# A new order of work per engine, pair sums on VectorE and a bf16 softmax in a two-branch token-mixing kernel

## The chip, the cores and the metric

One Trainium2 chip, one core. The metric is the device time of one execution in microseconds (us). Before the change it was 210.38 us (median of 3 runs, 210.28 to 210.64). The executions of before agree within about 0.3%. A run that is more than 1.5% above the fastest run of the same kernel is called slow and kept out of the comparisons.

Engine names: PE is TensorE (matmuls), PEld its weight loads, DVE VectorE, ACT ScalarE, POOL GpSimd, SP SyncE, which here only issues transfers.

## The reference, cut to what matters

```python
# x (1, 2048, 512) bf16; 32 heads of 16; window of 8 keys, dilation 2; Fh = 688
xn = layernorm(x)
# A: local attention
q, k, v = split(xn @ wqkv)                       # per head
logits[s, w] = q[s] . k[s - 2*w] / 4,  w = 0..7  # masked where s - 2*w < 0
o = softmax(logits) applied to v[s - 2*w];  A = o @ wo
# B: gated mixing over the tokens
z = gelu(xn @ w_in);  z1 = z[:, :688];  z2 = layernorm(z[:, 688:])
g = w_sp @ z2 + b_sp                             # w_sp is 2048 x 2048: the largest product
B = (z1 * g) @ w_out
out = x + A + B
```

The kernel works on 16 tiles of 128 tokens. "Tile n" below is the n-th in the kernel's own order.

## The kernel before: the parts that matter

The logits are made by DVE, which multiplies q by shifted k over all 512 channels, and by PE, which adds up each head's 16 channels with a 0/1 matrix. The channels lie in four chunks of 128, so each group of logits takes four passes of PE.

```python
NWSP = 6                                   # homes for transposed tiles of w_sp
NZ1 = 8                                    # slots for z1 and u = z1 * g
...
def logits(g):
    pl = ps_aux.tile([P, 4, P], F32, name="pl", tag="aux")
    for c in range(C):                     # C = 4 chunks
        for tb in range(TB):
            PE.matmul(pl[32 * tb:32 * tb + 32, :, :], rsel[:, c, :], pr[g % 2][:, c, :, tb, :],
                      start=(c == 0), stop=(c == C - 1), tile_position=(0, 32 * tb))
    A.activation(lg[:, 4 * h:4 * h + 4, o, :], pl[:], ACT.Copy, scale=float(DH) ** -0.5)
```

The gelu of z1 tile n writes slot n % 8. `u_mul` multiplies g into the same slot. A DMA transpose on SP's queue then reads that slot into `uT`, from where PE uses it as weights:

```python
def z1_mm(n):
    pz = zmm(i, w_z1)                                      # PE, into a PSUM buffer (3 of them)
    A.activation(z1u[:, n % NZ1, z:z + FH]..., pz[:, :, 0:FHALF], ACT.Gelu_apprx_tanh)

def u_mul(n, gs):
    s = n % NZ1
    V.tensor_tensor(z1u[:, s, 0:FULL], g[:, 0:FULL], z1u[:, s, z:z + FULL], ALU.mult)
    ...
    SP.dma_start_transpose(uT[:, (n // 4) % 2, :, ...], z1u[:, s, :])   # directly behind the multiply
```

The order is a plain program. The weights `wo` (2 MB in all, because four copies go to four partition groups) are issued ahead of the loop:

```python
for tb in range(TB):
    SP.dma_start(wo_r[32 * tb:32 * tb + 32, :, :], A_wo.rearrange("(h d) n -> h d n", d=DH))
load_xr(0)
...
for n in range(NT):
    if n >= 4:
        z1_mm(n)
    gs = g_mm(n)
    if n in OUT_AFTER: outs(n)             # an output block of 4 tiles, then its next residual loads
    for _ in range(APPLY_PER_G[n]):
        ap.pop(0)()                        # attention applies on DVE
    u_mul(n, gs)
    ...
    if n + NWSP < NT:
        load_wsp(n + NWSP)                 # DMA transpose of one tile of w_sp
out_mm(3, last=True)
```

## Time and profile before

| | value | where |
|---|---|---|
| time | 210.38 us, span of the profiled run 209.3 us | runs, page |
| PE busy | 202.7 us, 97% | page, part 1 |
| first q/k matmul | 8.46 us | timeline |
| last matmul ends | 206.0 us, 3.3 us before the end | stretches |
| DVE, ACT busy | 176.9, 92.9 us | page, part 1 |

Three lines of the page before: busy time of each engine with its share of the span and number of instructions; then the span in 40 slices, a digit for the busy tenths of PE and of the clock that the throttle granted it.

```profile
PE 202.7 (97%) x1727; PEld 121.3 (58%) x1731; DVE 176.9 (85%) x267; ACT 92.9 (44%) x148; POOL 5.7 (3%) x21
...
PE   7799999999999999999999999999999999999993
...
PEclk9999999999999999999999999999999999999999
```

Busy time in three stretches of before, cut at the first q/k matmul and at the last matmul. Columns: stretch and its length, busy us of PE, PEld, DVE, ACT, POOL (instructions), mean granted clock, DMA share, GB/s.

```profile
0.00:8.46 8.46, 5.87 (x19) 2.17 (x20) 4.56 (x15) 3.09 (x6) 4.41 (x19) 1.00 0.67 203
8.46:206.00 197.54, 196.79 (x1708) 119.12 (x1711) 171.60 (x250) 89.81 (x143) 1.29 (x2) 1.00 0.57 120
206.00:209.30 3.30, 0.00 (x0) 0.00 (x0) 0.76 (x2) 0.00 (x0) 0.00 (x0) 0.90 0.37 119
```

Read the middle line first: of 197.54 us PE is busy 196.79, at full clock. PE is the limit from end to end, so only two things can shorten this kernel: less work on PE, or shorter ends. Everything else has slack, and slack can only be lost.

The group of the logits matmuls before (engine, operation, tiles, shapes, count, busy us, mean ns, idle before):

```profile
L304 PE MATMUL pl<-r_pr,rsel 128*32 128x512 bf16 x128 | 8.2, 381 | 0.0
```

The queue of SP before, around the issue of `wo`. Columns: start, duration of the issue, queue, line, operation, transfer, count.

```profile
89.63 2.92 SPq L609 DMA_DIRECT2D r_lg<-in_A_wo_dram  x4
92.60 1.91 SPq L397 DMA_DIRECT2D r_qk<-in_A_x_dram  x4
102.63 1.28 SPq L392 DMA_TRANSPOSE uT<-z1u  x1
104.02 1.96 SPq L369 DMA_TRANSPOSE r_qk<-in_B_w_sp_dram  x1
```

`wo` goes out at 89.6 us, 42 us before the output heads use it (131.39 us). The two durations of a transpose: 1.28 us for a tile of u, 1.96 us for a tile of w_sp.

### The profile page before, as it was taken

What the parts mean: (1) busy time and instruction counts of PE and PEld (TensorE: products, weight loads), DVE (VectorE), ACT (ScalarE), POOL (GpSimd) and SP (SyncE); (2) the same over time, 40 slices, a digit from 0 to 9 for tenths busy, and PEclk for the clock granted to TensorE, in tenths of its full rate; (3) what the DMA queues carried; (4) which work ended last, traced back from release to release, by engine and by line L of the source; (5) the groups of instructions that cost most, each with busy time, mean ns of one, the idle gap of its engine ahead of it and who ended that gap; (6) DMA issues with size and microseconds to landing.
All of it is one profiled execution on the core that took longest, in us unless ns stands there. A gap on an engine that the chain in (4) does not pass through costs nothing.

```text
span 209.3 us, 4186 instructions
## 1 busy us (share of the span) xinstructions
PE 202.7 (97%) x1727; PEld 121.3 (58%) x1731; DVE 176.9 (85%) x267; ACT 92.9 (44%) x148; POOL 5.7 (3%) x21
## 2 busy tenths in 40 slices
PE   7799999999999999999999999999999999999993
PEld 2578644545566566666666666456666446664441
DVE  3888997969999987999999999859999979991404
ACT  3475797788997897941431223102123102231000
POOL 7000001100000000000000000000000000000000
PEclk9999999999999999999999999999999999999999
DMA  4984556000000499799999776994833234424153
GB/s 132 326 281 66 101 94 232 0 0 3 0 3 0 103 179 210 146 280 216 177 191 218 129 161 145 147 194 150 126 76 89 47 94 150 47 45 89 51 152 100
DMA packets 66914, 25.91 MB, mean 124 GB/s; under 512 B 56080, under 2 KB 66768, under 8 KB 66768
## 3 DMA queue, kind: packets, MB, share of 16 engines
q1 hardware_dynamic: 66304, 25.20, 56.1%
q10 hardware_dynamic: 592, 0.46, 0.7%
q8 instruction: 13, 0.21, 0.4%
q14 instruction: 5, 0.04, 0.1%
HBM read 10.13 MB, written 2.10 MB: 58 GB/s over the span
## 4 chain that ended last, share of the span: by engine, by line
PE 93%; DMA 3%; SPq 2%; issue 1%; DVE 0%; DVEq 0%
PE pg L377 36%; PE pz L207 18%; PE pq L264 12%; PE po L430 7%; PE po L411 7%; PE pv L342 7%; PE pl L304 4%; DMA r_w<-in_A_wqkv_dram 3%; PE pa L430 1%; PE po L417 1%; SPq L138 1%; SPq L131 1%; SPq L147 0%; PE pt L193 0%; DVE r_qk L422 0%
## 5 line engine op out<-in xcount | busy, mean ns | idle before, releaser
L377 PE MATMUL pg<-z,r_qk 128*128 128x344 bf16 x512 | 76.8, 309 | 0.0
L377 PEld LDWEIGHTS <-r_qk 128*128 128x128 bf16 x512 | 50.0, 98 | 24.9 <-issue 0.4
L207 PE MATMUL pz<-w_z,xnT 128*128 128x344 bf16 x256 | 40.9, 309 | 0.0
L380 ACT ACTIVATE gs<-pg,b_col 128x688 bf16<-128x688 f32 x16 | 13.3, 832 | 57.0 <-PE pg L377 50.1
L353 DVE TENSOR_TENSOR r_pr<-r_x,r_w 128x2048 bf16<-128x2048 bf16 x32 | 38.1, 1221 | 0.3
L357 DVE TENSOR_TENSOR r_pr<-r_pr 128x2048 bf16<-128x2048 bf16 x28 | 33.8, 1219 | 0.1
L207 PEld LDWEIGHTS <-xnT 128*128 128x128 bf16 x256 | 24.6, 98 | 14.7 <-issue 2.0
L264 PE MATMUL pq<-xnT,r_w 128*128 128x256 bf16 (+1 forms) x176 | 29.4, 321 | 0.8 <-ACT xnT L197 0.7
L297 DVE TENSOR_TENSOR r_pr<-r_qk 128x2048 bf16<-128x2048 bf16 x24 | 27.5, 1218 | 2.8 <-ACT r_qk L269 2.8
L264 PEld LDWEIGHTS <-r_w 128*128 128x128 bf16 x176 | 16.8, 98 | 11.5 <-issue 1.8
L422 DVE TENSOR_TENSOR r_qk<-po,r_qk 128x512 bf16<-128x512 f32 x14 | 9.0, 686 | 15.6 <-PE po L430 15.6
L256 ACT ACTIVATE z1u<-pz 128x688 bf16<-128x688 f32 x16 | 11.9, 742 | 20.8 <-PE pz L207 20.7
L269 ACT CAST r_qk<-pq 128x1024 bf16<-128x1024 f32 x16 | 15.8, 1012 | 5.8 <-PE pq L264 4.3
L430 PE MATMUL po<-r_w,uT 128*128 128x512 bf16 x66 | 14.9, 379 | 0.6 <-issue 0.6
L342 PE MATMUL pv<-xnT,r_w 128*32 128x512 bf16 x256 | 14.7, 380 | 0.0
L411 PE MATMUL po<-r_lg,r_pr 32*128 32x512 bf16 x224 | 14.5, 375 | 0.0
L430 PEld LDWEIGHTS <-uT 128*128 128x128 bf16 x80 | 7.5, 98 | 10.2 <-issue 1.7
L175 DVE BATCH_NORM_STATS2 stats<-r_x 128x6 f32<-128x512 bf16 x16 | 10.8, 672 | 2.3 <-DMA r_x<-in_A_x_dram 2.1
L219 ACT ACTIVATE junk<-z 128x688 bf16<-128x688 bf16 x16 | 12.4, 778 | 0.5
L213 ACT ACTIVATE z<-pz 128x688 bf16<-128x688 f32 x16 | 11.8, 736 | 1.9 <-PE pz L207 1.9
L342 PEld LDWEIGHTS <-r_w 128*32 128x32 bf16 x256 | 9.5, 139 | 4.5 <-issue 0.3
L411 PEld LDWEIGHTS <-r_pr 32*128 32x128 bf16 x256 | 6.2, 93 | 7.7 <-issue 1.3
(67 smaller groups left out, 136.3 us busy)
## 6 DMA issues: line engine op xcount, KB each, us to landing
r_lg<-in_A_wo_dram SPq DMA_DIRECT2D x4, 512.0 KB, 9.0
r_qk<-in_A_x_dram SPq DMA_DIRECT2D x16, 128.0 KB, 2.2
out_dram<-r_qk SPq DMA_DIRECT2D x15, 128.0 KB, 1.7
r_x<-in_A_x_dram SPq DMA_DIRECT2D x3, 512.0 KB, 6.0
w_z<-in_B_w_in_dram SPq DMA_DIRECT2D x2, 688.0 KB, 5.3
r_w<-in_A_wqkv_dram SPq DMA_DIRECT2D x4, 256.0 KB, 6.4
r_w<-in_B_w_out_dram SPq DMA_DIRECT2D x1, 640.0 KB, 5.6
r_w<-in_A_wqkv_dram SPq DMA_DIRECT2D x1, 512.0 KB, 4.0
```

Source lines behind the costliest of these rows:

```text
L207: PE.matmul(pz[:, hh, 0:FHALF], xnT[:, kc, i * P:(i + 1) * P], wz[:, kc, hh * FHALF:(hh + 1) * FHALF], start=(kc == 0), stop=(kc == C - 1))
L219: A.activation(junk[:], z2[:, i, :], ACT.Square, accum_out=zsq[:, q:q + 1])
L264: PE.matmul(pq[:, s, b0 * P:b1 * P], wqk[:, kc, s * D + c * P:s * D + (c + 1) * P], xv[:, kc, b0:b1, j, :], start=(kc == 0), stop=(kc == C ...
L269: A.copy(dst[:, :, :, j, :], pq[:].rearrange("p s (b t) -> p s b t", b=TB))
L297: V.tensor_tensor(pr[g % 2][:, :, ww], q4, k4, ALU.mult)
L342: PE.matmul(pv[32 * tb:32 * tb + 32, dd, :], wv[:, kc, 2 * d2 + dd, :], xnT[:, kc, tb * TBS:(tb + 1) * TBS], start=(kc == 0), stop=(kc == ...
L353: V.tensor_tensor(pw_t[n], vp[:, :, off:off + P], a_sb[:, slot_w(w), ts].unsqueeze(1).broadcast_to([P, DH, P]), ALU.mult)
L357: V.tensor_tensor(pw_t[n] if dst is None else dst, pw_t[n], pw_t[m], ALU.add)
L377: PE.matmul(pg[:, hh, 0:FHALF], wsp[n % NWSP][:, k, :], z2[:, k, hh * FHALF:(hh + 1) * FHALF], start=(q == 0), stop=(q == NT - 1))
L380: A.activation(gs[:], pg[:, :, 0:FHALF], ACT.Identity, bias=b_col[:, i:i + 1])
L411: PE.matmul(pos[tb], op[32 * tb:32 * tb + 32, d, o * P:(o + 1) * P], wo_r[32 * tb:32 * tb + 32, d, :], start=(d == 0), stop=False, tile_po ...
L430: PE.matmul(pos[tb], uT[:, o % 2, m, tb * P:(tb + 1) * P], wout[:, m, :], start=False, stop=(m == MCH - 3))
```

## The change

The intent: halve PE's work for the logits, which is PE time, by letting DVE first add the four chunks in pairs; make room on DVE with a bf16 softmax and with a reciprocal taken on ACT as exp(-ln); and place every single step of z2, q/k, softmax, v, g, applies and outputs by a list, so that PE always finds its inputs. The w_sp tiles get separate homes. As before, `wo` can be issued only after the second softmax exponential, because its home is the logits' buffer; that exponential now ends at about 119 us. The bf16 logits fill only the lower half of the buffer, and two w_sp tiles use the upper half for a time.

```diff
-NWSP = 6
-APPLY_PER_G = [1, 2, 3, 4, 4, 4, 4, 4, 4, 6, 6, 6, 4, 4, 3, 1]
-OUT_AFTER = [8, 12, 15.5]
+PAIRED = (0, 1, 2, 3, 4, 5, 6, 7)
+ORDER = """
+z0.2 z0.3 z2.2 zg0.2 p1.3 ...
+... A9 M1.1 U1 M1.2 Gi3 A10 G5 Gi9 M1.3 U3 E1 A11 T3 A12 wo X8 Gi5 S1.0 X11 A13 w11 G8 A14 Xg8 Xg11 A15 xr0 A16 U6
+T2 A17 X9 Gi8 T1 U5 S1.1 G7 A18 A19 Xg9 S1.2 A20 A21 O0 Gi7 A22 ... A24 Or0 Oh0.0 A25 U8 Oh0.1 F0.0
+A26 s0.0 w10 U7 G11 ... A31 G12 A32 xr1
+Gi10 A33 A34 T7 A35 T5 A36 X15 Gi12 s0.3 T9 A37 X12 A38 X14 Xg15 A39 Xg12 G15 ...
+... xr3 Or3 Oh3.0 Oh3.1 F3.0 F3.1 s3.1 s3.0
+"""
 NZ1 = 8
...
+    def pair_add(g):
+        V.tensor_tensor(pr[g % 3][:, 0:2], pr[g % 3][:, 0:2], pr[g % 3][:, 2:4], ALU.add)
...
-        for c in range(C):
+        n_c = 2 if g in PAIRED else C
+        for c in range(n_c):
             for tb in range(TB):
-                PE.matmul(pl[...], rsel[:, c, :], pr[g % 2][:, c, :, tb, :],
+                PE.matmul(pl[...], rsel[:], pr[g % 3][:, c, :, tb, :],
...
-        V.reciprocal(s4[:, 0, :], s4[:, 0, :])
+            A.activation(smt[:, 1, :], smt[:, 0, :], ACT.Ln)
+            A.activation(srec[:], smt[:, 1, :], ACT.Exp, scale=-1.0)
...
-    for c in range(C):
-        prod_c(0, c)
...
+    for tok in ORDER.split():
+        name = tok.rstrip("0123456789.")
+        steps[name](*[int(a) for a in tok[len(name):].split(".") if a])
```

Words of the list: `Xn` z1 matmuls of tile n, `Xgn` their gelu, `Gn` g matmuls, `Un` multiply, `Tn` DMA transpose of tile n of u, `wn` DMA transpose of tile n of w_sp, `wo` the four loads of wo, `xro` the residual loads of output block o, `Oo`, `Oro`, `Oho.h` the matmuls of output block o, `Fo.t` and `so.t` its adds and stores. Each engine takes its own steps in the order of the list; dependences between engines are added automatically. `T1`, `wo`, `w11`, `xr0` and `T2` all go through SP.

## The prediction

> **What bounds the kernel now.** TensorE. The page has PE busy 202.7 of 209.3 us, and by its waits PE never idles more than 0.2 us at a time after its first q/k matmul at 8.46 us. The stretches view: 59.97 of 59.98 us busy from 23.5 (first z2 tile) to 83.5 (first g tile), 121.8 of 122.5 from there to 206.0. Behind the last matmul is a tail of 3.3 us (add, store). Clock 1.0 throughout. DVE is busy 176.9 us, ACT 92.9 us. So only PE work removed, or the two ends, can give time; moves on other engines can only cost.
>
> **Removed from PE.** The logits reduction: 128 matmuls, 8.2 us (0.98 per group of 16). Pair sums halve them: -4.1 us. Nothing else on PE shrinks; 256-column halves and the cut last block add about 0.3 us.
>
> **Start.** The second transpose no longer stands behind two warm-up matmuls (they end at 7.35; its input was ready at 6.35), and the q weights come as one transfer issued about 0.9 us earlier. First q/k matmul perhaps 0.4 us earlier (0 to 0.7).
>
> **DVE.** Eight adds of 4096 elements: a 2048-element bf16 operation has a pitch of 1.14 us, so 2.2 each, +17.7. bf16 max, subtract and normalise at half the fp32 cost (1.22 against 2.29 us for 2048; the Trainium skill, "VectorE: DVE Perf Modes", has 2-byte tensor_tensor at two elements a cycle; the trace agrees): -6.9; reciprocal moved to ACT -3.5; one Newton chain less -2.5. DVE grows by about 5 us to 181 while the span shrinks: nearly critical.
>
> **ACT.** 10 table loads for 4. The skill ("ScalarE: Activation LUTs", What ACT_TABLE_LOAD costs) says 2.66 us with the drain; this trace shows 1.28 us and the next instruction directly after. +7.7 us, plus small Ln/Exp; ACT has room, but loads delay PSUM evacuations.
>
> **New waits.** Adding up the new order per engine with these durations, DVE first waits for q/k casts (blocks 2, 0, 3) and falls some 7 us further behind. Then: a few tenths at L5 and G0 (pair sum, z2 norms), about 1 us at L6/L7 (pair sum 7), about 0.8 at the second-last output block (uT transpose queued on SP behind the one for tile 13), little or nothing at the last head projection, which the final apply add reaches barely in time, and perhaps at O0 (2 MB of wo issued only near 99+ us). Together 2 us (1 to 5).
>
> **Tail.** On DVE the adds of the first two tiles of the last block now stand *behind* the three adds of the last two, and their two 128 KB stores leave last on SP. After the last matmul come one 224-column add, two 0.66 us adds, two issues of 0.65 us, a transfer: about 5.3 us instead of 3.3, +2 us.
>
> **Sum.** 210.4 - 4.1 - 0.4 + 0.3 + 2.0 + 2 = 210.2; I may overestimate waits, for such an order is presumably searched for: 209.2 us, 8 in 10 from 206.3 to 212.3. Faster by 2%: 0.12; within: 0.80; slower: 0.08.
>
> **What would show it.** PE busy near 199; logits group near 4.1 us; PE idle of 1 to 5 us released by DVE pair adds, z2 norms or DMA; DVE busy near 181; 10 table loads; last matmul to end about 5.3 us with two DVE adds in it.
>
> **What would make it wrong.** DVE lag larger than added up (mask, strided product slower than 1.22 us, apply adds): then all outputs slip, slower. Later x arrival through the GpSimd queue. Or no waits and an earlier start: 207.

## The result, and the profile after

The change made the kernel slower: 218.95 us (218.81, 216.94, 219.21, 219.10) against 210.51 us for before in the same rounds, a ratio of 1.0367, 95% interval 1.0318 to 1.0415. A ratio here and below is the mean time of one kernel's fast runs over that of the other's in the same rounds, so it is not quite the ratio of the medians quoted. All outputs were correct.

The same three lines of the page after:

```profile
PE 201.7 (93%) x1695; PEld 126.7 (58%) x1699; DVE 181.1 (83%) x259; ACT 100.0 (46%) x161; POOL 3.4 (2%) x15
...
PE   8899999999999999999999995499996999999990
...
PEclk9999999999999999999999999599999699999999
```

PE has two dents, at about 60% and 80% of the span, and the granted clock has one at or just behind each. Outside them PE is as full as before. What PE waited for after (engine, line, releaser: us in total, times, longest):

```profile
PE po L495 <- ACT r_uz L296: 5.4, 1, 5.4
PE pg L447 <- ACT r_uz L296: 2.4, 1, 2.4
```

Two waits, 7.8 us, both for an instruction of line 296, the gelu of z1. What that gelu waited for:

```profile
ACT r_uz L296 <- DMA r_uz<-r_uz: 9.9, 1, 9.9
```

`r_uz<-r_uz` is a DMA transpose of u: it reads a slot of u in `r_uz` and writes `uT`, in the same tensor. The queue of SP after shows why it was late; these are the lines that answer to the four of before:

```profile
117.76 1.22 SPq L467 DMA_TRANSPOSE r_uz<-r_uz  x1
119.20 1.79 SPq L642 DMA_DIRECT2D r_lg<-in_A_wo_dram  x4
121.09 10.45 SPq L438 DMA_TRANSPOSE r_qk<-in_B_w_sp_dram  x1
131.58 2.00 SPq L472 DMA_DIRECT2D r_qk<-in_A_x_dram  x4
133.63 2.56 SPq L467 DMA_TRANSPOSE r_uz<-r_uz  x2
```

The third line is the event. The issue of one w_sp transpose, 1.96 us before, held SP's queue for 10.45 us. (A wait for a semaphore lies ahead of an issue's start and is not part of this time: in e2 below an issue of 0.32 us follows a wait of 20 us.) The four `wo` transfers, issued just ahead, landed at 125.24, 127.59, 130.18 and 131.84 us; the issue ended at 131.54. The two transposes in the last line are `T2` and `T1`; `T1` landed at 137.66. Then, in time order on the other engines (start, duration, engine, line, operation; the bracket is the idle time before and what ended it):

```profile
127.95 4.83 PE L447 MATMUL pg<-z,r_qk 128*128 128x344 bf16 x32
132.71 0.39 PE L495 MATMUL po<-r_lg,r_pr 32*128 32x512 bf16 x2
137.74 0.74 ACT L296 ACTIVATE r_uz<-pz 128x688 bf16<-128x688 f32 x1 [9.87 <-DMA r_uz<-r_uz]
138.53 5.29 PE L495 MATMUL po<-r_lg,r_pr 32*128 32x512 bf16 x62 [5.44 <-ACT r_uz L296]
146.56 0.69 DVE L509 TENSOR_TENSOR r_qk<-po,r_qk 128x512 bf16<-128x512 f32 x1 [7.68 <-PE po L519]
```

Gelu 9 writes slot 9 % 8 = 1, so it must wait until `T1` has read that slot. Until gelu 9 has read its PSUM buffer, the buffer is not free. There are three of them: z1 tile 9, g tile 7, and the first of two for the output heads. After two head matmuls PE stands, until gelu 9 is done. DVE later waits 7.68 us for the first output sums.

The second dent is the same dependence with n = 15 and slot 7. `T7` was issued from 162.92 us in a pair, behind the residual loads `xr1`, landed at 166.4, and ACT then still had a table to load (1.28 us) before the gelus. PE stood 2.41 us, until 168.60:

```profile
162.92 2.59 SPq L467 DMA_TRANSPOSE r_uz<-r_uz  x2
168.60 6.50 PE L447 MATMUL pg<-z,r_qk 128*128 128x344 bf16 x32 [2.41 <-ACT r_uz L296]
```

The stretches after, cut at the first q/k matmul, around the first dent, and at the last matmul:

```profile
7.37:132.80 125.43, 125.30 (x1058) 84.15 (x1058) 115.69 (x171) 83.62 (x139) 0.81 (x2) 1.00 0.55 119
132.80:138.50 5.70, 0.30 (x2) 0.00 (x1) 5.63 (x6) 0.76 (x2) 0.00 (x0) 0.70 0.74 183
138.50:212.10 73.60, 70.50 (x617) 40.58 (x620) 53.68 (x67) 12.61 (x16) 0.00 (x0) 0.95 0.50 107
212.10:217.10 5.00, 0.00 (x0) 0.00 (x0) 1.59 (x4) 0.00 (x0) 0.00 (x0) 0.99 0.33 105
```

Up to 132.8 us nothing was lost at all: PE is busy 125.30 of 125.43 us. The first g tile starts at 81.36 us, against 83.45 before, although 4.6 us more of z matmuls lie ahead of it (192 against 160) and only 16 of the 64 logits matmuls (1.0 us) are left for later. By this estimate the change was more than 5 us ahead at that point. In the clock's own records half rate was granted from 135.12 to 141.94 and from 169.25 to 172.66 us. In both stretches about 3.41 us of it lay under matmuls, which loses half of that: an estimate of 1.7 us each. The matmul times agree: the 62 head matmuls behind the first dent took 5.29 us, all 64 of them before 3.63.

The logits after, in two tiles because a third buffer was added:

```profile
L358 PE MATMUL pl<-r_pr,rsel 128*32 128x512 bf16 x48 | 3.3, 381 | 0.0
L358 PE MATMUL pl<-r_uz,rsel 128*32 128x512 bf16 x16 | 1.2, 382 | 0.0
```

3.3 + 1.2 = 4.5 us instead of 8.2: 3.7 us less. With the spans of the two profiled runs (209.3 and 217.1) the account is as follows. PE's work is what the other terms leave; PE's busy time in the same stretch, less the half clock, gives the same (196.10 - 3.4 - 196.79 = -4.1).

| term | us | from |
|---|---|---|
| first q/k matmul earlier | -1.1 | 7.37 - 8.46 |
| PE work between first q/k and last matmul | -4.1 | (212.09 - 7.37 - 7.85 - 3.4) - 197.54; 3.7 of it logits |
| PE idle | +7.85 | 5.44 + 2.41 |
| half clock under matmuls | +3.4 | estimate from the clock records, as above |
| last matmul to the end | +1.7 | 5.0 - 3.3 |
| sum | +7.8 | 217.1 - 209.3 = 7.8 |

The start. Before, then after: the second group of transposes stood behind two warm-up matmuls; after, all eight run together.

```profile
6.29 1.06 PE L469 MATMUL pwm<-warm 128*128 128x512 bf16 x2
7.41 0.38 PE L193 MATMUL pt<-ident,r_x 128*128 128x128 bf16 x4
8.46 1.03 PE L264 MATMUL pq<-xnT,r_w 128*128 128x256 bf16 x8 [0.67 <-ACT xnT L197]
```

```profile
5.78 0.92 PE L220 MATMUL pt<-ident,r_x 128*128 128x128 bf16 x8 [0.27 <-DVE r_x L213]
6.53 0.49 PE L546 MATMUL pwm<-warm 128*128 128x512 bf16 x2
7.37 1.03 PE L305 MATMUL pq<-xnT,r_w 128*128 128x256 bf16 x8 [0.35 <-ACT xnT L224]
```

The end. Before, two additions of 256 columns are left after the last matmul, which ends at 205.97 us. After, the last matmul ends at 212.09 us; one addition of 224 columns follows, then two of 512 columns, and their stores behind them:

```profile
206.01 0.76 DVE L422 TENSOR_TENSOR r_qk<-pa,r_qk 128x256 bf16<-128x256 f32 x2 [0.27 <-PE pa L430]
```

```profile
212.12 0.39 DVE L509 TENSOR_TENSOR r_qk<-pb,r_qk 128x224 bf16<-128x224 f32 x1
212.43 1.28 DVE L509 TENSOR_TENSOR r_qk<-po,r_qk 128x512 bf16<-128x512 f32 x2
```

### The profile page after: what moved, and what is told of

Same layout as the page of the kernel before. It is cut to its first block, busy times and chain, and to the rows that moved or that the text cites. A ratio compares the mean times of both kernels' runs of the same rounds, so it can differ in the third digit from the quotient of the medians.

```text
span 217.1 us, 4082 instructions
## 1 busy us (share of the span) xinstructions
PE 201.7 (93%) x1695; PEld 126.7 (58%) x1699; DVE 181.1 (83%) x259; ACT 100.0 (46%) x161; POOL 3.4 (2%) x15
## 3 DMA queue, kind: packets, MB, share of 16 engines
HBM read 10.13 MB, written 2.10 MB: 56 GB/s over the span
## 4 chain that ended last, share of the span: by engine, by line
PE 78%; DVE 8%; DMA 6%; SPq 4%; issue 1%; ACT 1%; DVEq 0%; ACTq 0%
PE pg L447 27%; PE pz L234 16%; PE pq L305 12%; PE po L495 7%; PE pv L408 6%; PE po L519 6%; DMA r_w<-in_A_wqkv_dram 3%; DVE r_pr L422 3%; DMA r_uz<-r_uz 3%; DVE r_pr L426 2%; PE pl L358 2%; DVE r_qk L509 2%; SPq L438 2%; SPq L472 1%; PE pa L519 1%
## 5 line engine op out<-in xcount | busy, mean ns | idle before, releaser
L447 PE MATMUL pg<-z,r_qk 128*128 128x344 bf16 x448 | 68.1, 314 | 2.4 <-ACT r_uz L296 2.4
L447 PEld LDWEIGHTS <-r_qk 128*128 128x128 bf16 x448 | 44.4, 99 | 25.4 <-issue 2.6
L305 PEld LDWEIGHTS <-r_w 128*128 128x128 bf16 x184 | 20.1, 114 | 7.6 <-DMA r_w<-in_A_wqkv_dram 0.8
L315 ACT CAST r_qk<-pq 128x1024 bf16<-128x1024 f32 (+1 forms) x16 | 15.3, 991 | 4.9 <-PE pq L305 4.9
L296 ACT ACTIVATE r_uz<-pz 128x688 bf16<-128x688 f32 x16 | 11.5, 744 | 12.1 <-DMA r_uz<-r_uz 9.9
L495 PEld LDWEIGHTS <-r_pr 32*128 32x128 bf16 x272 | 8.4, 99 | 13.2 <-issue 8.7
L519 PE MATMUL po<-r_w,r_uz 128*128 128x512 bf16 x66 | 14.9, 379 | 0.6 <-issue 0.6
L350 DVE TENSOR_TENSOR r_pr<-r_pr 128x4096 bf16<-128x4096 bf16 x6 | 13.7, 2284 | 0.1
L519 PEld LDWEIGHTS <-r_uz 128*128 128x128 bf16 x85 | 8.0, 98 | 9.8 <-issue 1.5
L339 DVE TENSOR_TENSOR r_uz<-r_qk 128x2048 bf16<-128x2048 bf16 x8 | 9.7, 1220 | 3.3 <-ACT r_qk L315 3.3
```

What stands on the lines that cost most here:

```text
L305: PE.matmul(pq[:, cc, p0 * P:(p0 + b1 - b0) * P], wqk[:, sd, kc, c0 + cc:D:C], xv[:, kc, b0:b1, j, :], start=(kc == 0), stop=(kc == C - 1))
L315: cast = A.copy(dst, pq[:, :, p0 * P:(p0 + b1 - b0) * P].rearrange("p c (b t) -> p c b t", b=b1 - b0))
L339: prod = V.tensor_tensor(pr[g % 3][:, c].rearrange("p w b t -> p b w t"), q3.unsqueeze(2).broadcast_to([P, TB, 4, P]), k4, ALU.mult)
L350: V.tensor_tensor(pr[g % 3][:, 0:2], pr[g % 3][:, 0:2], pr[g % 3][:, 2:4], ALU.add)
L447: PE.matmul(pg[:, hh, 0:FHALF], wsp[n][:, k, :], z2[:, k, hh * FHALF:(hh + 1) * FHALF], start=(k == 0), stop=(k == NT - 1))
L495: PE.matmul(pc, op[32 * tb:32 * tb + 32, d, o * P:(o + 1) * P], wo_r[32 * tb:32 * tb + 32, d, cs], start=(d == 0), stop=False, tile_positi ...
```

## The experiments

Theory A: the slowdown comes from u transposes that stand too late in SP's queue, the first of them behind a w_sp transpose that the 2 MB of `wo` holds up; gelu, PSUM buffer and PE follow. Rival B: DVE is overloaded by the pair sums (181 us busy) and everything slips behind it. Rival C: the long w_sp transpose waited for PE, as the profile infers (it names z1 matmuls of line 234 as its releaser, 7.1 us; the z1 tile that ends in that time is the one that runs from 126.78 us), and `wo` has nothing to do with it. A further question is how much the order of the end costs. Ten kernels ran, all correct. The first four share one chip and its runs of before, so do e5 to e8, and so do e9 and e10. Times in the table are medians of the fast runs; one run of e1, two of e2 and one of e10 count as slow.

| run | edit, against the kernel after unless said | time us | ratio to before, 95% |
|---|---|---|---|
| after | | 218.95 | 1.0367 (1.0318 to 1.0415) |
| e1 | T2, T1 ahead of wo | 211.28 | 1.0057 (0.9996 to 1.0118) |
| e2 | wo issued by ACT | 231.02 | 1.0975 (1.0926 to 1.1024) |
| e3 | adds of the end reordered | 215.82 | 1.0281 (1.0226 to 1.0335) |
| e4 | e1 and e3 | 209.17 | 0.9939 (0.9924 to 0.9954) |
| e5 | e4, T7 and T5 early | 207.30 | 0.9839 (0.9819 to 0.9859) |
| e6 | e5 without pair sums | 210.89 | 1.0004 (0.9983 to 1.0026) |
| e7 | e5, wo in two halves | 205.55 | 0.9757 (0.9741 to 0.9774) |
| e8 | no pair sums, order as given | 220.75 | 1.0477 (1.0441 to 1.0513) |
| e9 | w11 behind T1 | 215.71 | 1.0220 (1.0156 to 1.0284) |
| e10 | wo in two halves, order as given | 212.59 | 1.0155 (1.0089 to 1.0221) |

### e1: two transposes ahead of wo

```diff
-... E1 A11 T3 A12 wo X8 ... A16 U6
-T2 A17 X9 Gi8 T1 U5 S1.1 G7 ...
+... E1 A11 T3 T2 T1 A12 wo X8 ... A16 U6
+A17 X9 Gi8 U5 S1.1 G7 ...
```

> The change as given, but the transposes of u tiles 2 and 1 stand on the SyncE queue ahead of the wo loads and of the w_sp load for tile 11; nothing else moves. Theory A (queue order: gelu 9 must wait until the transpose of u tile 1 has read its buffer, and that transpose stood behind a w_sp load whose issue took 10.45 us while 2 MB of wo were in flight): the 9.9 us wait of ScalarE for that transpose, the 5.4 us idle of TensorE before the first head projection and the 7.7 us wait of VectorE for the first output add go; the clock stays at 1.0 there; 208 to 213 us against 219. The second stall (2.4 us before g tile 15, behind the residual loads of block 1) may stay or shrink. Theory B (VectorE is overloaded by the pair adds and everything runs late): at most 1 us better, 217.5 or more.

211.28 us (211.28, 213.26, 210.58; a fourth, 215.25, counts as slow), against 218.95. The wait of the output heads for a gelu is gone. One wait of 1.5 us for `wo` itself and the wait at tile 15 (3.2 us) are left. The profiled run of this kernel is the slow one: it holds two stretches of half clock, and I read only the kinds of waits from it. The held w_sp transpose was still there, 10.58 us long (10.13 in e4 below). So the hold alone made PE wait for no gelu; what stood behind it did. This supports A and speaks against B, since DVE's work is the same.

### e2: wo through the other issuing engine

```diff
-            SP.dma_start(wo_r[32 * tb:32 * tb + 32, :, :], A_wo...)
+            A.dma_start(wo_r[32 * tb:32 * tb + 32, :, :], A_wo...)
```

> The change as given, but the four wo loads go out from ScalarE's queue; the order on SyncE's queue is unchanged. Theory A (the w_sp load for tile 11 is held at issue by the wo bytes in the same queue): its issue takes 2 to 4 us instead of 10.45, the transpose of u tile 1 is issued before 128 us of the span, the stall before the first head projection shrinks to under 1 us, 208 to 214 us. Rival C (that w_sp load waits for TensorE, as the profile's inference says: g tile 5 or the z1 tile that ends at 128.1): the load still ends near 131.5 us and the time stays within 1 us of 219.

231.02 us (230.21 and 231.83; the other two, 233.68 and 234.51, count as slow): the time missed both expectations by far, and `T1` went out at 137.5 us instead of before 128. The transpose itself answered the question. The queue of SP in e2:

```profile
119.67 3.51 SPq L438 DMA_TRANSPOSE r_qk<-in_B_w_sp_dram  x1
123.23 12.02 SPq L472 DMA_DIRECT2D r_qk<-in_A_x_dram  x4
```

It was issued by 123.18 us, in 3.51 us, although the z1 tile that C lets it wait for did not run before 142 us in this kernel (PE had stopped at 122.0). C falls, and an inferred releaser is only an inference: the hold has to do with `wo`. (The home of this w_sp tile is that of tile 5, and g tile 5, its last reader, was through at 119.9 us in the kernel after.) That `wo` must stand in the same queue is not shown, because ACT had sent off only two of the four transfers, half of the bytes, by the time the transpose was through.

The loss came from elsewhere. ACT did no work for 22.83 us, and PE idled 20.6 us at one place. The four issues themselves took only 0.32 to 0.43 us each. In the trace the third and the fourth wait for a semaphore, the counter that a transfer raises when it lands, which had last been given to a transfer of SP's queue: the third went out at 140.87 us, when the w_sp transpose had landed at 140.84, the fourth at 141.22, when the first residual load had landed at 141.18. The Trainium skill, "DMA: Bandwidth & Descriptors", section "Issuing engines are not separate DMA queues", says that transfers of all issuers interleave on the same 16 DMA engines and that using several issuers saves only sequencer time, "which is usually small". The second half agrees with these short issues, of transfers that took 5.4 to 20.5 us to land. The first half is not tested here: the residual loads beside `wo` took 12.02 us to issue, against 2.00, but they stood behind the w_sp transpose in their own queue.

### e3: the end

```diff
-... xr3 Or3 Oh3.0 Oh3.1 F3.0 F3.1 s3.1 s3.0
+... xr3 Or3 Oh3.0 F3.0 F3.1 s3.1 s3.0 Oh3.1
```

> The change as given, but the adds and stores of the first two tiles of the last output block stand before the matmuls and adds of the last two. All theories: from the last matmul to the end 3.3 to 3.6 us instead of 5.5, so 2.0 us faster (216.5 to 217.2); the stalls in the middle stay.

215.82 us (215.84, 215.80, 215.77, 218.24). The last matmul to the end is 3.4 us (210.7 to 214.1) instead of 5.0. (The 5.5 in the expectation came from a cut at 211.6 us, ahead of the last matmul.) The ratio fell by 1.0367 - 1.0281 = 0.0086, about 1.8 us. The medians differ by more, 3.1 us: in three of the four runs the mean granted clock was 0.984, against 0.975 to 0.978 in the kernel after, and the profiled one has no half clock behind its second dent. Both dents stay (5.6 and 1.3 us). So the end was a separate loss, of 1.6 us by the trace.

### e4: both repairs

> Both edits of order (u transposes 2 and 1 early; tail adds early). Theory A: the sum of the two gains, 206 to 211 us, at or under the kernel before (210.4). Theory B: 215 or more.

209.17 us (209.00 to 209.49), ratio 0.9939: both repairs add up, and the granted clock is 1.00 throughout. The queue of SP in e4, where `T2` and `T1` are already gone before `wo`:

```profile
117.41 3.91 SPq L467 DMA_TRANSPOSE r_uz<-r_uz  x3
121.43 1.91 SPq L642 DMA_DIRECT2D r_lg<-in_A_wo_dram  x4
123.44 10.13 SPq L438 DMA_TRANSPOSE r_qk<-in_B_w_sp_dram  x1
```

A wait at tile 15 is left, now 2.3 us, and 1.0 us for `wo`.

### e5: the second late transpose

```diff
 # on top of e4
-A26 s0.0 w10 U7 G11 ...  /  Gi10 A33 A34 T7 A35 T5 A36 X15 ...
+A26 s0.0 w10 U7 T7 T5 G11 ...  /  Gi10 A33 A34 A35 A36 X15 ...
```

> The two edits of order of the run before it (u transposes 2 and 1 early, tail adds early), and the transposes of u tiles 7 and 5 directly after the products of tile 7, ahead of the stores and residual loads of block 0 to 1. Theory A: the last wait of TensorE on a u transpose (2.3 us before g tile 15) goes, the 1.0 us wait for wo stays: 206.4 to 207.4 us against 209.17 without it. Theory B (VectorE late): no change, 209.

207.30 us (206.91 to 207.67), ratio 0.9839. The wait at tile 15 is gone; 1.2 us of waiting for `wo` is the only new wait left. So the second dent, too, was a u transpose issued late, and three moves of steps on SP and DVE have taken the kernel from 3.7% slower to 1.6% faster.

### e6: what the pair sums are worth

```diff
 # on top of e5
-PAIRED = (0, 1, 2, 3, 4, 5, 6, 7)
+PAIRED = ()
```

> The run before it with no pair sums: four chunks go into each logits matmul group again. If the pair sums are worth their TensorE time once nothing stalls: 4.1 us slower than e5 (210 to 211.5), minus up to 1 us if VectorE's 18 us less brings wo earlier. If VectorE were what bounds (theory B): the same as e5 or faster.

210.89 us, ratio 1.0004. Against e5 of the same rounds: (1.0004 - 0.9839) x 210.7 = 3.5 us. PE busy rises from 197.5 to 201.1 us, DVE falls from 180.9 to 163.6. PE's saving arrives in the total nearly whole, once nothing else stands in the way; DVE's 17.3 us cost nothing. The expectation that `wo` would come earlier with less work on DVE missed: it went out at 124.22 us, 121.63 in e5, and PE's wait for it grew from 1.2 to 1.8 us, so up to 0.6 of the 3.5 us may be this wait.

### e8: no pair sums in the given order

Edit: `PAIRED = ()` in the kernel after, nothing else.

> The change exactly as given, but no pair sums. Theory A: the queue order is unchanged, so gelu 9 still waits for the transpose behind the w_sp load behind wo; VectorE reaches the softmax of the second half earlier, so wo goes out up to 8 us earlier and the stall shrinks by what wo gains, while TensorE has 4.1 us more: 212 to 220 us. Theory B: VectorE's lag was the cause, so the stall is gone and the time is 209 to 212 us, TensorE never idle over 1 us.

220.75 us (2 runs), just above the 212 to 220 of theory A; ratio 1.0477. What PE waited for in e8:

```profile
PE po L495 <- ACT r_uz L296: 5.8, 1, 5.8
```

DVE was relieved of 17.4 us (163.7 busy), and the stall of 5.4 us became 5.8. B falls. One part of my own expectation missed: with DVE freed I thought `wo` would go out earlier; it went out at 121.98 us, later than with the pair sums (119.20), probably because PE then has 4 us more logits work ahead of it.

### e9: the w_sp transpose moved behind the u transposes

```diff
-... wo X8 Gi5 S1.0 X11 A13 w11 G8 ... xr0 A16 U6 T2 A17 X9 Gi8 T1 U5 ...
+... wo X8 Gi5 S1.0 X11 A13 G8 ... xr0 A16 U6 T2 A17 X9 Gi8 T1 w11 U5 ...
```

> The change as given, but the w_sp load for tile 11 stands behind the transpose of u tile 1 on SyncE's queue; wo and the four residual loads still stand ahead of it. If only the many small descriptors of a transposing load are held behind the 2 MB of wo: the residual loads and the transpose go out without delay, its landing is before 129 us, the stall before the first head projection is gone, 208 to 213 us. If whatever is issued next behind wo is held until wo has mostly moved: the residual loads or the u transposes take the 8 to 10 us instead, the stall stays over 3 us, 216 to 219 us.

215.71 us (215.38, 216.04, 213.07, 216.18), ratio 1.0220. This asks whether the w_sp transpose is special, or whether any DMA transpose directly behind `wo` is held. The queue of SP in e9:

```profile
118.85 1.79 SPq L642 DMA_DIRECT2D r_lg<-in_A_wo_dram  x4
120.68 2.37 SPq L472 DMA_DIRECT2D r_qk<-in_A_x_dram  x4
123.98 8.00 SPq L467 DMA_TRANSPOSE r_uz<-r_uz  x2
```

The plain residual loads behind `wo` went out in 2.37 us. The u transposes behind them were held, 8.00 us for two instead of 2.56, until 131.98 us; the last `wo` transfer landed at 131.41. So a transpose of u is held as well, not only one of w_sp, and plain loads in this place are not. (In e2 plain loads were slow too, behind a w_sp transpose.) Neither branch of the expectation came true as written: the residual loads went out freely, the u transposes did not, and with a stall of 2.7 us the time lay just under the second branch.

### e10: wo in two halves, in the given order

```diff
-... M1.0 w7 U2 ...  A11 T3 A12 wo X8 ...
+... M1.0 w7 wo.1 U2 ...  A11 T3 A12 wo.0 X8 ...
-    def load_wo():
+    def load_wo(h):
         for tb in range(TB):
-            SP.dma_start(wo_r[32 * tb:32 * tb + 32, :, :], A_wo.rearrange("(h d) n -> h d n", d=DH))
+            SP.dma_start(wo_r[32 * tb:32 * tb + 32, 8 * h:8 * h + 8, :],
+                         A_wo.rearrange("(h d) n -> h d n", d=DH)[:, 8 * h:8 * h + 8, :])
```

The upper half of wo's home becomes free before the exponential and is loaded earlier, so only 1 MB goes out directly ahead of the w_sp transpose.

> The change as given, but wo in two halves, the first issued about 7 us earlier; the queue order of the u transposes is not touched. If the hold grows with the wo bytes still in flight: the issue of the w_sp load for tile 11 takes about 5 us instead of 10.45, the transpose of u tile 1 goes out 5 us earlier, the stall before the first head projection shrinks from 5.4 us to under 1.5 us, and without a stretch of half clock there: 211 to 215 us. If the hold does not depend on it: within 1 us of 219.

212.59 us (211.57, 212.59, 213.27; a fourth, 215.49, counts as slow), ratio 1.0155. The queue of SP in e10: `T3` between the two halves of `wo`, and the w_sp transpose behind the second:

```profile
117.51 1.22 SPq L467 DMA_TRANSPOSE r_uz<-r_uz  x1
121.54 6.54 SPq L438 DMA_TRANSPOSE r_qk<-in_B_w_sp_dram  x1
```

Half the bytes directly ahead, and the hold shrinks to 6.54 us, from 10.45 (9.99 to 11.34 in the seven profiled runs where the whole of `wo` stands there). I had expected about 5, but when this issue began two transfers of the first half were still on their way (landed at 121.79 and 122.79 us), so more than 1 MB was in flight. In e7, where the first half had landed before, it took 5.22 us. The first stall is 2.5 us, where I had expected under 1.5. Direction right, size off.

`T3` is worth a look: it went out in 1.22 us, without any hold, while all four transfers of the first half were in flight (they landed at 119.39 to 122.79 us). The profiled run had no stretch of half clock, so here 2.5 + 1.8 us of idle cost no more than themselves.

### e7: the version that beats both

Edit: e5 with the halves of e10.

> e5 with wo loaded in two halves: the half whose home is free after g tile 3 is issued about 7 us before the other. The 1.0 us wait of TensorE for wo before the first head projection goes: 0.5 to 1.2 us faster than e5. If the DMA is simply busy all through that stretch: no change.

205.55 us (205.41 to 205.78), ratio 0.9757: 2.4% faster than before. Against e5 that is (0.9839 - 0.9757) x 210.7 = 1.7 us, more than the 0.5 to 1.2 expected; e5's wait for `wo` was 1.2 us, and where the rest comes from was not looked into. The hold in e7, and its page:

```profile
125.63 5.22 SPq L438 DMA_TRANSPOSE r_qk<-in_B_w_sp_dram  x1
```

```profile
PE 197.0 (97%) x1695; PEld 125.2 (61%) x1699; DVE 180.9 (89%) x259; ACT 100.3 (49%) x161; POOL 3.5 (2%) x15
...
PEclk9999999999999999999999999999999999999999
```

PE no longer waits for `wo`, for a gelu or for anything else in its middle; the only waits over 0.6 us are the two at the start (1.1 us each, both inside the warm-up). With 197.0 us of work PE is as full as before, at a lower total.

## Why the prediction was wrong

It named 209.2 us and a range to 212.3; it became 218.95. Point by point:

- **Bounds: right.** PE is the limit. Every us that PE idled was lost; the 7.7 us that DVE stood still (between 138.9 and 146.6) were only a consequence.
- **Logits: right in kind, close in size.** -4.1 predicted, -3.7 in the groups; 3.5 us shown as the worth of the pair sums by e6 against e5.
- **Start: undersized.** -0.4 (0 to 0.7) predicted, -1.1 measured. The timelines show the transposes freed from the warm-ups, as predicted; how much is due to the transfers was not tested.
- **DVE: right.** 181 predicted, 181.1 measured. Its pair sums took 2.28 us each where I had estimated 2.2, and the bf16 subtraction of 2048 elements 1.21 us, as the two elements a cycle of the Trainium skill ("VectorE: DVE Perf Modes", section "Side-by-side: where the cycles go for N=2048 bf16") led me to expect.
- **ACT: right.** Ten table loads of 1.283 us each, and not the 2.66 us that the Trainium skill ("ScalarE: Activation LUTs", section "What ACT_TABLE_LOAD costs") gives with the drain. One load of 1.28 us does sit inside the second stall.
- **Tail: right.** 5.3 predicted, 5.0 measured; e3 gave back 1.6 us by reordering it.
- **PE work otherwise: close.** I had added 0.3 us for smaller matmuls; the account shows about 0.4 us less beyond the logits. Which edits did that is open.
- **New waits: this step failed.** The prediction has "Together 2 us (1 to 5)", named as waits for q/k casts, pair sums and z2 norms, for a transpose of u at the second-last output block, and perhaps for `wo`. PE shows none of them: from its first q/k matmul to 132.8 us it lost 0.13 us in all, and behind that its only waits over 0.2 us are the two for a gelu. In their place the runs showed 7.85 us of idle and about 3.4 us of half clock, 11.3 in all, from one dependence that was not on my list: gelu n must wait until the transpose of tile n - 8 has read the slot. The prediction's own list of what would make it wrong had a larger lag of DVE at its head; e8 shows that it was not this.

Two things went wrong in that step. First, I followed forward dependences (who needs this result) and left out the backward one (who must have finished reading before this buffer is written again). In the kernel before, each transpose was issued right behind its multiply, seven tiles before the slot's next use, so this edge never showed in the trace. Second, I costed every transfer with the duration it had in the trace of before, where the next transpose went out only at 102.63 us, when the last of `wo` was about to land (103.10). The prediction did look at `wo` ("perhaps at O0", issued "near 99+ us"); it went out at 119.2 us, and waiting for it cost PE 1.0 to 1.8 us in e1, e4, e5 and e6. But it looked only at who consumes `wo`, not at what stands behind it in the same queue.

Of the difference between 218.95 and 209.2, this term accounts for 11.3 - 2 = 9.3 us. The start (-0.7), PE's work (-0.3), the tail (-0.3) and 1.0 us that I had taken off the sum as a discount for a searched order leave about 0.8 us unexplained; the account is that of two profiled runs, whose spans differ by 7.8 us where the medians differ by 8.4.

What is shown, and what is not: that the order of the u transposes causes the stalls is shown by e1, e4 and e5, which remove them one after the other. That the `wo` bytes ahead hold the transpose is shown by e9 and e10 together with e2: other transposes in the same place are held too, and fewer bytes of `wo` mean a shorter hold. *Why* it is held is not settled, but the traces narrow it down. In the ten profiled runs of the new order with `wo` on SP's queue the issue of the last held transpose ended between 0.6 us before and 0.6 us after the landing of the last `wo` transfer. This looks like a wait for the plain transfers to land, but it is not so for every transpose: `T3` in e10 went out in 1.22 us with four `wo` transfers in flight ahead of it, and in e9 the issue of the first of the two held transposes was over at 126.81 us, with two `wo` transfers still to land (128.91 and 131.41). A lack of room in the queues fits both, but no run measures such room.

Idle time can cost more than itself. After 5.4 to 5.8 us of idle the clock records show 6.83 us of half rate, after 20.6 us (e2) 20.48, and after 2.1 to 2.7 us either 3.41 us (after, e9) or none (e4, e10). The Trainium skill, "TensorE: Matmul & The Clock Gate", section "Part 1: The HAM clock gate", says that the clock halves after at least one idle window of 3413 ns, and that the window runs freely. The lengths of 3.41 and 6.83 us agree with that window. That a stall of 2.1 us was once enough does not fit "at least one idle window" read as idle throughout.

## What to carry to other kernels

When steps are moved, list for every buffer not only who waits for its content but who must have read it before it is written again, and through which queue that reader goes; a DMA transpose is such a reader, and it should be issued right behind its producer. Never cost a transfer by a quiet trace if the new order puts a large load ahead of it in the same queue; move what is urgent ahead of the large load, or split the load so that part of it goes out earlier. A change that saves time on the bounding engine can look like a failure when one stall hides it: undo the stall, not the saving, and measure again.

## What the Trainium skill lacked or had wrong

- "DMA: Bandwidth & Descriptors", section "Rules for kernel authors", says "A transpose next to ordinary DMAs needs nothing". For correct results that agrees with all runs here. For time it does not: a DMA transpose issued behind 2 MB of plain loads held its queue for 10.45 us (1.96 us otherwise), behind 1 MB 5.22 us (e7), while plain loads in the same place took 2.37 us for four. A u transpose behind the first 1 MB of e10 was not held (1.22 us). Neither this page nor the part on DMA instructions in "Perfetto Trace Analysis" gives a rule or a cost for this on this chip.
- No page was found to warn that a transfer can wait at its issue for the landing of another queue's transfer that was given the same semaphore before it. In e2 this kept ACT from computing for 22.8 us, while its four issues took 0.32 to 0.43 us each.
- "TensorE: Matmul & The Clock Gate", section "Part 1: The HAM clock gate": half rate came after idle times of 2.1 to 2.7 us in some runs (3.41 us of half rate each), and not after 2.3 and 2.5 us in others. The page's condition of one idle window of 3413 ns does not say what share of a window counts as idle.
- "ScalarE: Activation LUTs", section "What ACT_TABLE_LOAD costs": the page gives 1283 ns for the load, which agrees with 1.283 us for each of the ten here, and 1380 ns of drain on top, which the trace does not show: in eight of the ten cases the next activation begins within 0.02 us of the load's end, and in the other two it waits for another engine or a DMA.
